# Four p_k buffers, go_o ahead of gs_t, and a new layout and order around the output stage of a gated S4/SwiGLU layer with its gradients

## The chip, the cores and the metric

The kernel runs on one core of a Trainium2 chip. The metric is the device time of one execution in microseconds, as the median of the runs; a time is compared with that of the kernel before.

## The reference, cut to what matters

The layer normalises u (2048 tokens x 576 channels), sends it through a state-space convolution (a kernel K of 2048 taps for each channel, from 128 complex rates) and through a SwiGLU network (576 to 4608 and back), and multiplies both. Besides the output it returns the gradients of the input and of every parameter.

```
def _A_ref(u, A_re, A_im, B_re, B_im, C_re, C_im, log_dt, Dskip):
    dt = exp(log_dt)[:, None]
    logdA = dt * (A_re + 1j * A_im);  dB = dt * (B_re + 1j * B_im)
    P = exp(logdA[:, :, None] * arange(L))
    K = einsum("dn,dnl,dn->dl", C_re + 1j * C_im, P, dB).real
    y = irfft(rfft(u padded to 2L) * rfft(K padded to 2L))[:L]      # per channel
    return y + u * Dskip

def _B_ref(x, w1, w3, w2):
    return (silu(x @ w1) * (x @ w3)) @ w2

xn = layernorm(A_u)
s = _A_ref(xn, ...)
g = silu(_B_ref(xn, w1, w3, w2))
out = A_u + s * g
# returned: out and the vector-Jacobian product of grad_out for A_u, the eight
# S4 parameters, w1, w3 and w2
```

## The kernel before

**Stages.** Times are those of the profiled execution. A prologue (to some 95 us) normalises and makes tables and exponentials. Then three things run interleaved until some 525 us: the *gates* (72 steps of two token tiles by 512 hidden columns: products with w1 and w3 into pg and pu, Silu, the product h, and stores of g, u and h to H_dram, U_dram, G_dram), the *kernel generation* (36 chunks of 16 channels), and the *convolution* in two halves of the channels. The output stage (`ffn_output`, 496 to some 680 us) multiplies H by w2 for 16 token tiles and forms the output and two gradients of the gating. The backward stage (to some 1345 us) runs 18 groups of 256 hidden columns beside the convolution's gradient; the last stage (`phase6_inputs`) forms the input's gradient for 16 token tiles, with the sums for the parameters (`param_half`) between its products.

**Order.** A framework traces the instructions and orders them for each engine by a priority, which `self.at(us)` sets as a due time, and by the dependences; after that each engine and each DMA queue runs strictly in that order. `issue_after` adds an order on one engine without a wait. The gates are laid among the chunks and the convolution by `gate_time` (due times) and `gate_mark` (the chunk or transform whose products a gate must follow on TensorE). `BACK` places the inverse transforms of the convolution's later blocks behind certain gates.

**Memory.** Pools are stacked: a pool opened where an earlier one was closed takes its bytes, and its tiles wait for the last users of the tiles that lay there. The output stage lies on the bytes of the gates and the convolution, and small `gap` pools shift what follows. For the convolution the stack is, from its floor: spectra of u (u_0 to u_3), of the kernel (k2_0 to k2_3), raw spectra (kraw, two buffers), V (two), cm_t (two), s_t (three), ev (two).

**What the change touches.**
- `kgen_chunk` makes p_k and q_k on DVE and stores them to PZ_dram and Q_dram from SP; p_k comes from a pool of two buffers (`sb`), q_k from one of four (`qvp`). `kgen_sum` sums on TensorE, copies to k_s on ACT and spreads k_s over KT on POOL.
- `conv_half` transforms KT in four blocks (`dft_block`: two products, an ACT copy of one to ev, DVE's sum and difference), multiplies the spectra on DVE into V (`cmul_acc`) and transforms back (`idft_side`).
- In `ffn_output`, `begin` loads a tile of H transposed from SP (hcA, hcB, hcC in turn) by the pieces and gates in `marks` for tiles 0 to 2, and in one piece later; `finish` does the sigmoid and the gradients on DVE: go_o stays in SBUF, gs_t is stored to GS_dram from SP, o0 to the output. `turn_go` transposes go_o on TensorE; the framework placed it by its priority and its inputs.
- `param_half` takes two buffers of et_ps from a pool of three PSUM banks; DVE multiplies and reduces each (L1507, L1510).

Of the kernel before, what the change touches and what calls it, by code (L numbers as in the profile page):

```python
# [17 lines left out]
P = 128  # L18
# [82 lines left out]
class K:  # L101
# [25 lines left out]
    def pool(self, **kw):  # L127
        return self.tc.tile_pool(reuse_waits="tile", **kw)
# [617 lines left out]
    def kgen_chunk(self, ch, E, lhs, SEL, sb, qvp, ps):  # L746
# [17 lines left out]
        q = qvp.tile([P, 2, DC // 2, 2 * BV], BF16, name="q_k")  # L764
        p = sb.tile([P, 4, 2, 4, AV], BF16, name="p_k")
        rows = lambda a_: a_.rearrange("p (g d) -> p g d", g=4)
# [200 lines left out]
    def ssm_conv(self, T0, TC, ps, ps1):  # L967
        with self.pool(name="c_u", bufs=1) as up, \
                self.pool(name="c_k", bufs=1) as kp, \
                self.pool(name="c_raw", bufs=2) as rp, \  # L970
                self.pool(name="c_y", bufs=2) as ypool, \
                self.pool(name="c_tmp", bufs=2) as tp, \
                self.pool(name="c_s", bufs=3) as spool, self.pool(name="c_e", bufs=2) as epool:
            self.s_stores = []
            for h in range(2):
                yield from self.conv_half(h, T0 + TC * h * 92, TC, kp, up, rp, ypool, tp, spool, epool, ps)

# [69 lines left out]
    def gate_mark(self, n):  # L1047
        i = n - self.LEAD
        if i < self.SPAN:
            return int(36 * i / self.SPAN + 0.5) - 1  # L1050
        h, k = divmod(i - self.SPAN, 17)
        return 36 + 8 * h + (-1, -1, 0, 0, 1, 1, 2, 3, 3, 4, 4, 4, 5, 5, 5, 6, 6)[k]

# [97 lines left out]
    def ffn_output(self, T0, TB):  # L1151
# [9 lines left out]
        with ExitStack() as es:  # L1161
# [3 lines left out]
                                                           op("epb"), op("gap5"))  # L1165
            hpc, hpc1, hp, ip4, epc, gap6 = op("hc"), op("hc1"), op("h"), op("st", 3), op("epc"), op("gap6")
            wps = [op(f"w{f}") for f in (24, 28, 32, 0)]
            ipx2 = op("in2x")
            psA, psB, psC = [es.enter_context(self.pool(name="o_ps" + n, bufs=1, space=bass.MemoryType.PSUM, side="right"))
# [3 lines left out]
            gap.tile([P, 5120], BF16, name="o_gap")  # L1173
            for g_, n_ in ((gap2, 128), (gap3, 128), (gap4, 1216), (gap5, 128), (gap6, 1152)):
                g_.tile([P, n_], BF16, name="o_gap2")
# [12 lines left out]
                     [(f, f + 6, 61 + f // 6) for f in range(0, FT, 6)],  # L1188
                     [(FC, FC + 9, 67), (FC + 9, FT, 68), (0, 9, 68), (9, FC, 69)]]
            w2a = self.ktp.tile([P, LT, D], BF16, name="w2a", tag="KT")  # L1190
# [51 lines left out]
            def finish(st):  # L1242
# [12 lines left out]
                got = go_o[:, i, :]  # L1255
                nc.vector.tensor_tensor(out=got, in0=gos[:], in1=e[:], op=ALU.mult)
                gs_t = ip.tile([P, D], BF16, name="gs_t")
                nc.vector.tensor_tensor(out=p4(gs_t[:]), in0=n4(go_t[:]), in1=n4(g[:]), op=ALU.mult)
                nc.sync.dma_start(out=self.GS_dram[:, :, i, :].rearrange("g p d -> p g d"),
                                  in_=gs_t[:].rearrange("p (g d) -> p g d", g=4))  # L1260
                if i >= LT - cfg.KT:
                    nc.scalar.copy(out=self.gs_end[:, i - LT + cfg.KT], in_=gs_t[:, 0:D // 4])
                nc.vector.tensor_tensor(out=n4(g[:]), in0=p4(s_t[:]), in1=n4(g[:]), op=ALU.mult)
                o0 = ip.tile([P, D], BF16, name="o0")
                self.epi.append(nc.vector.tensor_tensor(out=o0[:], in0=g[:], in1=x_t[:], op=ALU.add))
                nc.sync.dma_start(out=self.tok("out_0", i), in_=o0[:])
                if i < LT - 1:
                    self.turn_go(i, pst.tile([P, DT, P], BF16, name="ptr"))

# [13 lines left out]
            for i in range(2, LT):  # L1283
                st = begin(i)
                product(st, 0, FT)
                finish(st)
# [29 lines left out]
    def params_open(self, S_all, ps):  # L1316
        cfg = self.cfg
        self.sums = ExitStack()
        gkp = self.sums.enter_context(self.pool(name="g_k", bufs=1, side="right"))
        self.qp = self.sums.enter_context(self.pool(name="g_q", bufs=2, side="right"))  # L1320
        self.zp = self.sums.enter_context(self.pool(name="g_z", bufs=3, side="right"))
        self.prp = self.sums.enter_context(self.pool(name="g_pr", bufs=1, side="right"))
        self.S_all, self.ps_T = S_all, ps
        self.gz = []
        for i in range(3):
            z = gkp.tile([P, 2, 2, 2, 8, cfg.LT], BF16, name=f"gz{i}")
            self.nc.vector.memset(z[:], 0.0)
            self.gz.append(z)
        self.half = 0
        self.loaded = {}  # L1330

# [163 lines left out]
    def param_half(self, ch, dg, gK, qT, pz):  # L1495
        nc, AV = self.nc, self.cfg.AV
        T = [self.ps_T.tile([P, 2, 2, 2, 2, AV], FP32, name="et_ps") for _ in range(2)]
        for x in range(2):
# [474 lines left out]
    def phase6_inputs(self, T2, TX, wT, acts, pool):  # L1973
# [7 lines left out]
        with pool(name="l_sb", bufs=2) as sb, pool(name="l_s1", bufs=1) as s1, \  # L1981
                pool(name="l_sm", bufs=4) as sm, pool(name="x_ps", bufs=2, space=bass.MemoryType.PSUM) as ps:
            def rows(i, gxs, go_o1, queue):
# [262 lines left out]
```

## Time and profile before

| | us |
|---|---|
| median of three runs | 1682.55 |
| the runs | 1669.41, 1682.55, 1689.53 |
| the profiled execution | 1682.95 |
| its span, first to last instruction | 1681.0 |
| PE busy | 1577.1 (94%) |
| DVE busy | 1389.3 (83%) |
| ACT busy | 837.3 (50%) |

How to read the rows: an instruction row begins with its start and its length in us, counted from the span's start, then the engine (PE is TensorE's products, PEld its weight loads, DVE VectorE, ACT ScalarE, POOL GpSimd, SPq the queue of SyncE), the line of the kernel, output <- input with shapes, and xN for N merged into one row. In square brackets stand the idle time of that engine just before and what ended it. A row of the list of waits gives the total, the number and the longest. A row of the table by windows gives the stretch, its length, the busy time of each engine with the number of instructions, the clock granted to TensorE (1.00 is full), the share of the 16 DMA engines and the GB/s moved.

### The profile page before, as it was taken

To read this page: it belongs to the slowest core of one execution; us is meant where nothing else is said; L and a number is where in the kernel's file an instruction comes from. 1 tells how busy PE (TensorE), PEld (TensorE's weight loads), DVE (VectorE), ACT (ScalarE), POOL (GpSimd) and SP (SyncE) were. 2 spreads that over 40 slices of the span, in tenths; PEclk is the share of its full clock that TensorE was granted. 3 is DMA by queue.
4 is the path that set the end of the run, shared out by engine and by line. 5 is a ranking of instruction groups with operands and counts; after the bars stand their busy time and mean duration, and the time that the engine had idled before them with its cause. 6 is when DMAs were issued, how large, how long until landed. Compare 5 with 4: busy or idle time off the path is not lost. (4 is left out here: it accounts for less than half of the span.)

```text
span 1681.0 us, 34288 instructions
## 1 busy us (share of the span) xinstructions
PE 1577.1 (94%) x13275; PEld 1148.2 (68%) x13327; DVE 1389.3 (83%) x2150; ACT 837.3 (50%) x1517; POOL 475.4 (28%) x778
## 2 busy tenths in 40 slices
PE   5799989899997899999999999999999999999998
PEld 2454434344445677788888888888888877887876
DVE  9889988798973455798996999879999964788887
ACT  6789989666652112765656565556555401000001
POOL 7756756533242111011111111111111232213131
PEclk9999999999999999999999999999999999999999
DMA  7899999989799889758676665789999999999993
GB/s 238 298 337 368 376 347 383 322 271 310 246 212 220 213 195 218 229 168 244 189 181 203 199 198 159 213 227 284 247 240 239 234 243 227 252 226 238 243 208 75
DMA packets 621037, 408.57 MB, mean 243 GB/s; under 512 B 424554, under 2 KB 562234, under 8 KB 616266
## 3 DMA queue, kind: packets, MB, share of 16 engines
q1 hardware_dynamic: 565184, 274.01, 64.7%
q0 software_dynamic: 33472, 114.23, 21.0%
q10 hardware_dynamic: 22218, 18.14, 3.8%
q8 instruction: 104, 1.70, 0.4%
q14 instruction: 59, 0.48, 0.1%
HBM read 128.52 MB, written 189.06 MB: 189 GB/s over the span
## 5 line engine op out<-in xcount | busy, mean ns | idle before, releaser
L1948 PEld LDWEIGHTS <-xn_bf 128*128 128x128 bf16 x2304 | 224.4, 98 | 34.7 <-issue 8.5
L2002 PEld LDWEIGHTS <-acts 128*128 128x128 bf16 x1970 | 192.1, 98 | 47.9 <-issue 0.2
L1112 PEld LDWEIGHTS <-xnT 128*128 128x128 bf16 x1152 | 108.3, 98 | 139.2 <-issue 33.3
L1507 DVE TENSOR_TENSOR pr_q<-et_ps,pz 128x1024 f32<-128x1024 f32 x144 | 176.0, 1222 | 29.1 <-PE et_ps L1502 19.9
L1933 POOL DMA_DIRECT2D out_dram<-gw x72 | 47.2, 656 | 536.4 <-ACT gw L1950 310.0
L1510 DVE TENSOR_REDUCE S_all<-pr_q 128x32 f32<-128x1024 f32 x144 | 175.3, 1217 | 3.2
L1882 PE MATMUL ph<-w2T,goT 128*128 128x256 bf16 x1440 | 169.7, 273 | 1.6 <-ACT gh L1885 1.6
L1112 PE MATMUL pg<-wmB_w,xnT 128*128 128x512 bf16 x541 | 151.3, 381 | 13.4 <-DVE g_t L1131 11.3
L2002 PE MATMUL px<-wT,acts 128*128 128x288 bf16 x1242 | 161.0, 287 | 0.0
L1923 PE MATMUL pgw<-go_o,h_n 128*128 128x288 bf16 x1152 | 152.3, 286 | 1.1 <-ACT gw L1929 1.0
L1882 PEld LDWEIGHTS <-goT 128*128 128x128 bf16 x1440 | 139.2, 98 | 18.9 <-issue 3.1
L1112 PE MATMUL pu<-wmB_w,xnT 128*128 128x512 bf16 x566 | 151.3, 385 | 0.3
L1948 PE MATMUL pgw<-gu_n,xn_bf 128*128 128x256 bf16 x1152 | 133.5, 272 | 3.6 <-ACT gw L1929 3.1
L1923 PEld LDWEIGHTS <-h_n 128*128 128x128 bf16 x1152 | 111.9, 98 | 29.2 <-issue 2.1
L1948 PE MATMUL pgw<-gg_n,xn_bf 128*128 128x256 bf16 x1152 | 130.2, 273 | 0.4 <-ACT gw L1950 0.4
L1127 ACT ACTIVATE s_t<-pg 128x512 bf16<-128x512 f32 x144 | 88.2, 612 | 72.3 <-PE pu L1121 59.0
L1885 ACT CAST gh<-ph 128x512 bf16<-128x512 f32 x144 | 80.6, 589 | 82.6 <-PE ph L1882 75.3
L806 POOL COPY KT<-k_s 64x128 bf16<-64x128 bf16 x144 | 87.1, 605 | 57.2 <-ACT k_s L803 52.5
L2121 ACT ACTIVATE go<-gx 128x576 bf16<-128x576 f32 x15 | 10.2, 683 | 178.2 <-DVE gx L2071 169.4
L2002 PE MATMUL px<-wA,acts 128*128 128x288 bf16 x728 | 95.6, 287 | 0.0
L1132 ACT CAST u_t<-pu 128x512 bf16<-128x512 f32 x144 | 87.1, 605 | 7.7 <-PE pu L1112 7.2
L1141 POOL DMA_DIRECT2D G_dram<-g_t x72 | 51.5, 715 | 120.2 <-ACT g_t L1129 75.3
(331 smaller groups left out, 3196.5 us busy)
## 6 DMA issues: line engine op xcount, KB each, us to landing
H_dram<-h_t SPq DMA_DIRECT2D x72, 256.0 KB
U_dram<-u_t POOLq DMA_DIRECT2D x72, 256.0 KB, 5.7
G_dram<-g_t POOLq DMA_DIRECT2D x72, 256.0 KB, 5.2
Q_dram<-q_k SPq DMA_DIRECT2D x36, 512.0 KB
gg_n<-G_dram POOLq DMA_DIRECT2D x18, 1024.0 KB, 6.3
h_n<-U_dram POOLq DMA_DIRECT2D x18, 1024.0 KB, 8.7
GG_dram<-gg_n SPq DMA_DIRECT2D x36, 512.0 KB
GU_dram<-gu_n SPq DMA_DIRECT2D x36, 512.0 KB
```

Source lines behind the costliest of these rows:

```text
L806: nc.gpsimd.tensor_copy(out=KT[64 * hf:64 * hf + 64, :, ch // 9, h, d1:d1 + 8], in_=ks[64 * h:64 * h + 64, :, h, hf].rearrange("p d a -> p ...
L1112: ins = nc.tensor.matmul(pt[:], lhsT=xnT[:, c, ts], rhs=wm[w][:, c, :], start=(q == 0 and c == 0), stop=(q == 1 and c == nfull - 1))
L1127: nc.scalar.activation(out=s_t[:, :, q, :], in_=pgv, func=ACT.Silu)
L1132: self.gate_last = nc.scalar.copy(out=u_t[:, :, q, :], in_=puv)
L1141: self.u_stores[step] = nc.gpsimd.dma_start(out=dst[fb * ng:(fb + 1) * ng, :, i0:i0 + NT, :].rearrange("g p t f -> p g (t f)"), in_=src[:] ...
L1507: nc.vector.tensor_tensor(out=pr[:].rearrange("p r k e -> p r (k e)"), in0=T[x][:].rearrange("p z k h j a -> p (z k h j a)")[:, None].to_b ...
L1510: nc.vector.tensor_reduce(out=self.S_all[:].rearrange("p r (h c) -> p r h c", h=2)[:, :, :, d0:d0 + 2], in_=pr[:].rearrange("p r k (h j a) ...
L1882: self.pe_last = nc.tensor.matmul(ph[j][:, k, :].rearrange("p (a f) -> p a f", f=P), lhsT=lw, rhs=rh, start=(n == 0), stop=(n == nfull))
L1885: self.sc(lambda: nc.scalar.copy(out=gh[:, j], in_=ph[j][:]))
L1923: self.pe_last = nc.tensor.matmul(pgw[pi_][:, 0:pw], lhsT=hn[:, tt, fl * P:(fl + 1) * P], rhs=go_o[:, tt, po:po + pw], start=(tt == 0), st ...
L1948: self.pe_last = nc.tensor.matmul(pw_[:, 0:FG], lhsT=self.xn_bf[:, tt, c * P:(c + 1) * P], rhs=nat[:, tt, :], start=(tt == 0), stop=(tt == ...
L2002: self.pe_last = nc.tensor.matmul(px[pi_][:, 0:pw], lhsT=acts[i][:, ai, fi, :], rhs=w[:, po:po + pw], start=(n == 0), stop=(n == len(steps ...
```

## The change

Four places are edited together. p_k comes from the pool of four buffers. The second half of the convolution is due 88 instead of 92 units after the first, and the gates beside it follow a transform one step later in its list. In `ffn_output` the pools are ordered anew, so that hcB lies on the bytes of kraw and tile 2's two halves on those of V; the pieces of tile 2 follow gates 67, 68, 70 and 71; DVE makes go_o before gs_t and gs_t before the product for the output; and go_o of a tile is transposed after 19 of the 36 steps of the next tile (tiles 0 and 1 after 12 and 25 steps of tile 2). In the last stage every fourth et_ps comes from a PSUM bank of its own.

```
@@ kgen_chunk
-        p = sb.tile([P, 4, 2, 4, AV], BF16, name="p_k")
+        p = qvp.tile([P, 4, 2, 4, AV], BF16, name="p_k")
@@ ssm_conv
-                yield from self.conv_half(h, T0 + TC * h * 92, TC, kp, up, rp, ypool, tp, spool, epool, ps)
+                yield from self.conv_half(h, T0 + TC * h * 88, TC, kp, up, rp, ypool, tp, spool, epool, ps)
@@ gate_mark
-        return 36 + 8 * h + (-1, -1, 0, 0, 1, 1, 2, 3, 3, 4, 4, 4, 5, 5, 5, 6, 6)[k]
+        return 36 + 8 * h + (-1, -1, 0, 0, 1, 1, 2, 3, 3, 4, 4, 4, 5, 5, 5, 6, 6, 6)[k + h]
@@ ffn_output
-            hpc, hpc1, hp, ip4, epc, gap6 = op("hc"), op("hc1"), op("h"), op("st", 3), op("epc"), op("gap6")
+            epc, ipx2, gap6, hp, hpc, hpc1, ip4 = op("epc"), op("in2x"), op("gap6"), op("h"), op("hc"), op("hc1"), op("st", 3)
             wps = [op(f"w{f}") for f in (24, 28, 32, 0)]
-            ipx2 = op("in2x")
...
-            for g_, n_ in ((gap2, 128), (gap3, 128), (gap4, 1216), (gap5, 128), (gap6, 1152)):
+            for g_, n_ in ((gap2, 128), (gap3, 128), (gap4, 1216), (gap5, 128), (gap6, 704)):
...
-                     [(FC, FC + 9, 67), (FC + 9, FT, 68), (0, 9, 68), (9, FC, 69)]]
+                     [(0, 9, 67), (9, FC, 68), (FC, FC + 9, 70), (FC + 9, FT, 71)]]
...
-                nc.vector.tensor_tensor(out=got, in0=gos[:], in1=e[:], op=ALU.mult)
+                made = nc.vector.tensor_tensor(out=got, in0=gos[:], in1=e[:], op=ALU.mult)
                 gs_t = ip.tile([P, D], BF16, name="gs_t")
-                nc.vector.tensor_tensor(out=p4(gs_t[:]), in0=n4(go_t[:]), in1=n4(g[:]), op=ALU.mult)
+                with self.tc.issue_after(made.ins):
+                    made = nc.vector.tensor_tensor(out=p4(gs_t[:]), in0=n4(go_t[:]), in1=n4(g[:]), op=ALU.mult)
...
-                nc.vector.tensor_tensor(out=n4(g[:]), in0=p4(s_t[:]), in1=n4(g[:]), op=ALU.mult)
+                with self.tc.issue_after(made.ins):
+                    nc.vector.tensor_tensor(out=n4(g[:]), in0=p4(s_t[:]), in1=n4(g[:]), op=ALU.mult)
...
-                if i < LT - 1:
-                    self.turn_go(i, pst.tile([P, DT, P], BF16, name="ptr"))
+
+            def turn(i, after):
+                self.turn_go(i, pst.tile([P, DT, P], BF16, name="ptr"), after)
...
-                product(st, 0, FT)
+                f0 = 0
+                for k, f1 in ((0, 12), (1, 25)) if i == 2 else ((i - 1, 19),):
+                    turn(k, product(st, f0, f1))
+                    f0 = f1
+                product(st, f0, FT)
@@ params_open
+        self.ps_X = None
@@ param_half
-        T = [self.ps_T.tile([P, 2, 2, 2, 2, AV], FP32, name="et_ps") for _ in range(2)]
+        T = [(self.ps_X if self.ps_X and (2 * self.half + x) % 4 == 3 else self.ps_T).tile([P, 2, 2, 2, 2, AV], FP32, name="et_ps")
+             for x in range(2)]
@@ phase6_inputs
-                pool(name="l_sm", bufs=4) as sm, pool(name="x_ps", bufs=2, space=bass.MemoryType.PSUM) as ps:
+                pool(name="l_sm", bufs=4) as sm, pool(name="x_ps", bufs=2, space=bass.MemoryType.PSUM) as ps, \
+                pool(name="x_T", bufs=1, space=bass.MemoryType.PSUM) as self.ps_X:
```

## The prediction

> **What bounds the kernel now.** I read the page first, then the table by windows, then all idle time of PE in order of time, then the engine or queue behind each gap. The page says how much TensorE (PE) works.
>
> ```profile
> span 1681.0 us, 34288 instructions
> PE 1577.1 (94%) x13275; PEld 1148.2 (68%) x13327; DVE 1389.3 (83%) x2150; ACT 837.3 (50%) x1517; POOL 475.4 (28%) x778
> ```
>
> The windows (span, then busy time of PE, PEld, DVE, ACT, POOL, PE's granted clock, DMA share, GB/s) separate the stages:
>
> ```profile
> 126.00:336.00 210.00, 196.91 (x1372) 88.07 (x1394) 182.90 (x292) 181.58 (x362) 133.13 (x208) 0.98 1.03 359
> 252.00:294.00 42.00, 41.55 (x294) 18.50 (x298) 36.51 (x58) 39.11 (x79) 26.52 (x43) 1.00 1.03 383
> 328.00:406.00 78.00, 76.03 (x406) 34.30 (x410) 76.20 (x112) 53.54 (x112) 27.98 (x40) 1.00 0.93 294
> 418.00:491.00 73.00, 68.06 (x361) 30.79 (x365) 72.12 (x104) 48.90 (x102) 24.77 (x36) 1.00 0.77 252
> ```
>
> PE is the bound wherever it isn't kept waiting (41.55 of 42 us), so a PE gap that goes away shortens the kernel by its length, unless another engine is late next. In the convolution DVE is as full (76.20 of 78, 72.12 of 73), and in the kernel generation the DMA share is 1.03. I sort the edits by the gap that each can close. Second price of a gap: PE's clock halves behind it.
>
> ```profile
> 228.40:231.70 3.30, 3.30 (x17) 0.94 (x15) 2.89 (x6) 1.76 (x4) 0.72 (x1) 0.50 1.03 400
> ...
> 324.00:327.30 3.30, 3.30 (x12) 0.96 (x10) 0.83 (x2) 0.33 (x1) 2.09 (x3) 0.50 0.87 306
> 491.30:494.50 3.20, 3.20 (x14) 1.89 (x13) 1.47 (x4) 1.35 (x3) 2.13 (x3) 0.50 1.16 78
> 508.40:515.00 6.60, 3.36 (x15) 2.12 (x16) 2.03 (x3) 0.00 (x0) 4.21 (x6) 0.50 1.07 237
> 549.30:556.00 6.70, 4.45 (x21) 2.81 (x22) 3.53 (x6) 0.74 (x2) 1.61 (x3) 0.50 1.16 296
> 1634.70:1638.00 3.30, 3.30 (x16) 2.09 (x14) 3.07 (x4) 0.00 (x0) 0.90 (x2) 0.50 1.28 207
> ```
>
> PE's busy time in such a stretch, halved, is what the clock costs: 1.65 us at 228, 297 and 324 (three alike), 1.6 at 491, 1.7 at 508, 2.2 at 549, 1.65 at 1634. The Trainium skill ("TensorE: Matmul & The Clock Gate", section "Why this matters for your kernels") advises to keep idle gaps of PE under about 3 us, since a window of idle time halves the clock. By it the gaps of 2.09, 2.43 and 2.94 us below would be free of that price, and the sum would come to 1656; the trace halves the clock behind each of the three, so the rows are used.
>
> **1. Four p_k buffers.** p_k moves from a pool with two buffers to one with four.
>
> ```profile
> 212.87 0.81 PE L1112 MATMUL pg<-wmB_w,xnT 128*128 128x512 bf16 x3 [2.24 <-DVE g_t L1131]
> 227.38 0.81 PE L1112 MATMUL pg<-wmB_w,xnT 128*128 128x512 bf16 x3 [3.18 <-DVE g_t L1131]
> 296.06 0.92 PE L1112 MATMUL pg<-wmB_w,xnT 128*128 128x512 bf16 x3 [2.09 <-DVE g_t L1131]
> 323.06 0.59 PE L1112 MATMUL pg<-wmB_w,xnT 128*128 128x512 bf16 x2 [3.21 <-DVE g_t L1131]
> ```
> ```profile
> DVE p_k L767 <- DMA PZ_dram<-p_k: 9.5, 5, 2.5
> ```
> ```profile
> 222.81 0.69 DVE L767 TENSOR_TENSOR p_k<-cp_k,E_l 128x1024 bf16<-128x1024 bf16 x1 [2.76 <-ACT u_t L1132]
> ```
>
> PE waits for DVE to empty pg (g_t), and each of the four times DVE had just waited at L767 for the store of p_k two chunks back (the one at 222.81 is put down to an ACT copy that was already over; I count it with the five). Gaps 2.24 + 3.18 + 2.09 + 3.21 = 10.7 us, three half-clock stretches 5.0: ceiling 15.7. The store itself doesn't get faster; two more chunks of patience must be enough, and behind p_k stand E_l (four buffers, loaded ahead) and h_t (three). With a DMA share of 1.03 a part will come back there. Bounds 0 and 15.7; I take 9.
>
> The Trainium skill ("DMA: Bandwidth & Descriptors", "Where 436 GB/s comes from") puts the limit of HBM for one core at about 358 GB/s. By it this stage (359) could not go faster and the edit would bring nothing, 1660 in all; the row at 252 shows 383 for 42 us, so the trace doesn't agree with it as a ceiling. The mechanism stays as a rival.
>
> **2. Price of that move in SBUF.** The pools of the kernel generation grow by 4 x 2048 - 2 x 2048 = 4096 bytes, so by adding the tile sizes k_s shifts from 132608..134656 to 136704..138752 (counted from the floor that both stages share with the gates). The convolution's second ev buffer lies at 136704..137856: until now on free bytes, afterwards on k_s, whose last reader is POOL.
>
> ```profile
> 332.22 2.91 POOL L806 COPY KT<-k_s 64x128 bf16<-64x128 bf16 x4
> ```
> ```profile
> 329.01 0.45 DVE L903 TENSOR_TENSOR k<-et_ps,ev 128x288 bf16<-128x288 f32 x1
> ```
>
> The second pair of spectra (DVE, 329.0) would come after 335.1: some 6 us later, of which DVE fills about one with h_t. Queued behind the waiting ev copy on ACT are the gates' s_t, g_t, u_t. DVE is full from there to 406, so it isn't made up. Bounds 0 (the scheduler reuses the first ev buffer) and -8; I take -5.
>
> **3. Second half of the convolution sooner (L976, L1052).** Its last inverse transform stays behind gate 69 (BACK), its DVE work starts one gate earlier.
>
> ```profile
> 414.82 0.69 DVE L1135 TENSOR_TENSOR h_t<-s_t,u_t 128x1024 bf16<-128x1024 bf16 x1 [3.75 <-ACT u_t L1132]
> ```
> ```profile
> 490.89 0.86 PE L945 MATMUL et_ps<-V,cT 128*128 128x288 bf16 x4 [2.43 <-DVE V L963]
> ```
>
> DVE idles 3.75 us just before that half; filled, V is 3.75 us sooner, more than the 2.43 that PE waits. Gain 2.43 + 1.6 = 4.0; bounds 0 and 4.0, I take 4.
>
> **4. Layout and order in ffn_output.** By adding tile sizes, tile 1's H (hcB) lay partly on a V buffer; it now covers exactly the two kraw buffers, whose last reader ends before 442. Its six loads may so follow gates 61 to 66 instead of standing behind tile 2's.
>
> ```profile
> 440.95 0.75 DVE L914 TENSOR_TENSOR k<-kraw 128x1152 bf16<-128x1152 bf16 x1
> ```
>
> ```profile
> 443.79 36.43 SPq L1138 DMA_DIRECT2D H_dram<-h_t  x8
> ...
> 491.26 6.79 SPq L1803 DMA_TRANSPOSE hcC<-H_dram  x2
> 498.16 18.22 SPq L1803 DMA_TRANSPOSE hcB<-H_dram  x6
> ...
> 527.21 8.80 SPq L1803 DMA_TRANSPOSE hcA<-H_dram  x1
> ```
> ```profile
> 511.64 3.80 PE L1238 MATMUL po<-w2g,hcB 128*128 128x288 bf16 x16 [6.76 <-DMA hcB<-H_dram]
> 541.30 2.13 PE L1238 MATMUL po<-w2g,hcA 128*128 128x288 bf16 x16 [1.36 <-DMA hcA<-H_dram]
> 551.55 0.86 PE L1293 MATMUL ptr<-ident_bf,go_o 128*128 128x128 bf16 x5 [5.30 <-DVE go_o L1256]
> ```
> ```profile
> 548.73 0.76 DVE L1258 TENSOR_TENSOR gs_t<-go_t,g 128x576 bf16<-128x576 bf16 x1 [6.46 <-DMA GS_dram<-gs_t]
> ```
>
> First gap: 6.76 + 1.7 = 8.5 us, which I take whole, since the eight H stores leave SP nearly empty from 443 to 480. The next two, 1.36 + 5.30 + 2.2 = 8.9, hang on SP's queue: GS stores stand behind the full-tile transposes, gs_t has two buffers, and go_o stood behind gs_t. With go_o first, go_o no longer waits for that store. But tile 3's load must now come sooner, as the products before it do, behind tile 2's last two pieces. Bounds -4 and 8.9; I take 6.
>
> **5. go_o first, the transposes by hand.** The steady output tiles:
>
> ```profile
> 577.72 2.12 PE L1238 MATMUL po<-w2g,hcA 128*128 128x288 bf16 x16
> 579.68 2.98 PE L1238 MATMUL po<-w2a,hcA 128*128 128x288 bf16 x23
> 582.93 0.57 PE L1293 MATMUL ptr<-ident_bf,go_o 128*128 128x128 bf16 x5 [0.27 <-DVE go_o L1256]
> 583.43 1.28 PE L1238 MATMUL po<-w2a,hcA 128*128 128x288 bf16 x9
> ...
> 587.48 1.76 PE L1238 MATMUL po<-w2g,hcB 128*128 128x288 bf16 x13
> ```
> ```profile
> 580.12 0.75 DVE L1258 TENSOR_TENSOR gs_t<-go_t,g 128x576 bf16<-128x576 bf16 x1
> ...
> 582.12 0.75 DVE L1256 TENSOR_TENSOR go_o<-gos,e 128x576 bf16<-128x576 f32 x1
> ```
>
> A tile takes 587.48 - 577.72 = 9.76 us. 16 products take 1.96, so 72 take 8.82, the five transposes 0.50: 0.44 is lost waiting for go_o. Two DVE operations of 0.67 leave go_o's way, so it ends at 581.5; 38 products in, at 582.4, PE asks for it. The same gap comes 11 times (563 to 661): 4.8 us. gs_t and its store come 1.3 us later, hidden behind the next tile's products; if that cover is gone, as after the last tile, it may cost 1. Bounds 3.5 and 4.8; I take 4.8.
>
> **6. A fourth buffer for et_ps in the last stage (x_T).**
>
> ```profile
> 1534.13 0.38 PE L1502 MATMUL et_ps<-gz,qT 128*128 128x128 bf16 x4 [1.14 <-DVE pr_q L1507]
> 1633.59 0.38 PE L1502 MATMUL et_ps<-gz,qT 128*128 128x128 bf16 x4 [2.94 <-DVE pr_q L1507]
> ```
>
> 1.14 + 2.94 + 1.65 = 5.7 at most; DVE must still do the same reductions: 3 to 5.7, I take 5.
>
> **Sum.** 9 - 5 + 4 + 8.5 + 6 + 4.8 + 5 = 32.3 us off the profiled execution's 1682.95 (span 1681.0 and 1.95 around it): 1651. That execution stands 0.4 us from the median of the three runs, 1682.55, whose spread (1669.41 to 1689.53) is about 1%: less than 1% can't be told from no change.
>
> **Rivals.** (a) The DMA engines bound the kernel generation: the wait goes from p_k to E_l or h_t, term 1 is 0, 1660. For it: share 1.03, 359 GB/s; against: 383 at 252. Chance 0.2. (b) The load chain behind tile 2 takes tile 4's gain back: term 4's second part is -4 and a half-clock stretch of 1.7 is added, 1663. For it: one hcA load held SP 8.80 us; against: DMA has more room once hcB is gone from 498 on. Chance 0.15. (c) The change doesn't do what it says: hcB's loads still stand late on SP; 8.5 and 6 are lost, 1666. Chance 0.1. (d) Slower: the six loads that took 18.22 us of SP now stand between the H stores. Eight stores in 36.43 us are 4.55 a gate; three h_t buffers cover two gates, 9.1 us. If a stretch of loads holds SP for longer, DVE stands still on h_t, and DVE is the bound there: 18.2 - 9.1 = 9.1, again 13.6 - 9.1 = 4.5 with tile 2's four pieces, 1.6 of clock. With terms 1 and 3 gone, 2 at -8 and 4's second part at -4: 8.5 - 4 + 4.8 + 5 - 8 - 15.2 = -8.9, 1692. Against it: a piece held SP some 3 us, and gates lie between. Chance 0.05.
>
> **How the numbers follow.** The forecast, 1651, has 0.5. All ceilings with term 2 at 0 give 47.6, 1635; (a), (b) and (c) reach to 1666, and with the low ends of their other terms to some 1672. Range 1636 to 1672. 1% under the profiled time is 1666: the forecast and most of (a) and (b) lie below it, 0.78; within 1% 0.17; slower by over 1%, 0.05.
>
> **What would show it.** No wait of L767 for PZ_dram and no PE gap over 1 us before 330; the second ev copy behind KT's last copy; no PE gap at the last V; hcB's loads on SP before 490 and no gap at its first product; output tiles of 9.3 us; no pr_q wait over 1 us after 1500. A stop of DVE or ACT on E_l, h_t or g_t in its place, or a longer one for hcA, would make the forecast wrong.

## The result, and the profile after

| | before | after |
|---|---|---|
| median of four runs each, us | 1684.93 | 1662.09 |
| the runs | 1669.41 to 1689.53 | 1656.60, 1656.96, 1667.21, 1675.49 |
| the profiled execution: span | 1681.0 | 1673.7 |

The ratio is 0.9897 (95% interval 0.9849 to 0.9946): 1.0% faster. A later comparison gave 0.9886 (0.9836 to 0.9936), with twelve executions of the changed kernel from 1649 to 1701 us. The ratios leave out executions over 1.5% above the fastest of their kernel, seven of those twelve among them, while medians, lowest and highest are of all: there 1677.84 us against 1679.84 for before, only 0.1% apart. The profile shown is of the slowest of the first four, with a stop in it that point 8 below is about.

The page of the changed kernel, and its table by windows (the first three windows as shown for before, the fourth is the output stage):

```profile
span 1673.7 us, 34331 instructions
PE 1579.0 (94%) x13327; PEld 1149.9 (69%) x13327; DVE 1391.2 (83%) x2150; ACT 837.0 (50%) x1517; POOL 472.4 (28%) x778
```
```profile
126.00:336.00 210.00, 199.37 (x1395) 88.33 (x1393) 182.18 (x290) 183.17 (x365) 132.04 (x211) 0.98 1.03 360
328.00:406.00 78.00, 71.54 (x388) 32.58 (x388) 74.29 (x109) 49.51 (x103) 21.69 (x31) 1.00 0.97 298
418.00:491.00 73.00, 70.93 (x388) 33.04 (x388) 68.41 (x99) 48.03 (x100) 29.79 (x44) 1.00 0.95 280
500.00:660.00 160.00, 153.47 (x1242) 118.80 (x1241) 93.32 (x135) 36.67 (x68) 29.20 (x52) 0.99 0.95 221
```

PE is busier where its gaps were closed (199.4 for 196.9 us in the kernel generation, 70.9 for 68.1 in the second half of the convolution), but less busy at 328 to 406 (71.5 for 76.0): gaps have moved there. The DMA share in the kernel generation is 1.03 as before. In the output stage PE is busy 153.5 us at a clock of 0.99; before had there:

```profile
500.00:660.00 160.00, 143.07 (x1109) 106.33 (x1110) 77.77 (x115) 26.71 (x55) 29.28 (x51) 0.96 0.99 206
```

By how much the same instruction comes earlier in the profile after (kps are the sums of a chunk on PE, V the first product of the spectra, ph products of the backward stage):

| instruction | before | after | lead |
|---|---|---|---|
| first kps (no edit acts yet) | 109.57 | 108.13 | 1.4 |
| last kps of the kernel generation | 327.54 | 318.05 | 9.5 |
| first V on DVE | 333.52 | 331.96 | 1.6 |
| first output product | 496.24 | 488.11 | 8.1 |
| first product of hcB | 511.64 | 498.09 | 13.6 |
| sigmoid of output tile 2 | 540.03 | 529.63 | 10.4 |
| sigmoid of output tile 3 | 558.43 | 539.64 | 18.8 |
| sigmoid of output tile 14 | 665.89 | 642.20 | 23.7 |
| PE's wait in front of ph | 680.45 | 656.62 | 23.8 |
| wait for pr_q near 1330 | 1332.18 | 1324.01 | 8.2 |
| end of the span | 1681.0 | 1673.7 | 7.3 |

The lead grows to 23.8 us at the end of the output stage and falls to 8.2 at one place in the backward stage, which no edit touches. The PE gaps of the changed kernel that answer to those of before or are new and over 2 us, in order of time (timeline of PE; the wait of some 3 us for acts near 1370 and that of some 2 us for gz near 1405 are in both kernels):

```profile
275.95 1.86 PE L1112 MATMUL pu<-wmB_w,xnT 128*128 128x512 bf16 x4 [3.49 <-DMA wmB_w<-in_B_w_dram]
...
334.11 0.42 PE L898 MATMUL et_ps<-KT,fT 128*128 128x288 bf16 x2 [2.65 <-DVE k L905]
...
484.25 2.30 PE L945 MATMUL et_ps<-V,cT 128*128 128x288 bf16 x16 [0.59 <-DVE V L963]
...
512.59 0.65 PE L1237 MATMUL po<-w2g,hcA 128*128 128x288 bf16 x4 [3.38 <-DMA w2g<-in_B_w_dram]
...
534.71 0.57 PE L1299 MATMUL ptr<-ident_bf,go_o 128*128 128x128 bf16 x5 [0.51 <-DVE go_o L1255]
...
1258.07 3.31 PE L1956 MATMUL pgw<-gu_n,xn_bf 128*128 128x256 bf16 x16 [14.22 <-ACT gw L1937]
...
1652.69 0.60 PE L1595 MATMUL et_ps<-ident_f,ST 128*64 128x128 f32 x4 [3.36 <-DVE ST L1581]
```

Of before's gaps, 6.76 on hcB, 1.36 on hcA and 2.94 on pr_q are gone, those on V and go_o are down to 0.59 and 0.51, and of the four on g_t two short ones are left (0.92 at 232.25, 1.19 at 244.84). New are 3.49 on a weight load, 2.65 on k, 3.38 on w2g (a part of w2), 14.22 on gw and 3.36 on ST, and two shorter ones on V in the first half of the convolution (1.30 at 381.47, 1.83 at 403.49). Behind the first of them the clock is halved for 5 us (a row of the table by windows):

```profile
276.00:281.00 5.00, 5.00 (x28) 1.90 (x28) 1.29 (x2) 1.66 (x3) 0.45 (x2) 0.50 1.03 403
```

### The profile page after: what moved, and what is told of

It is laid out like the page before. It is cut to its first block, busy times and chain, and to the rows that moved or that the text cites. A ratio compares the mean times of both kernels' runs of the same rounds, so it can differ in the third digit from the quotient of the medians.

```text
span 1673.7 us, 34331 instructions
## 1 busy us (share of the span) xinstructions
PE 1579.0 (94%) x13327; PEld 1149.9 (69%) x13327; DVE 1391.2 (83%) x2150; ACT 837.0 (50%) x1517; POOL 472.4 (28%) x778
## 5 line engine op out<-in xcount | busy, mean ns | idle before, releaser
L1956 PEld LDWEIGHTS <-xn_bf 128*128 128x128 bf16 x2304 | 225.1, 98 | 50.6 <-issue 23.7
L1112 PE MATMUL pg<-wmB_w,xnT 128*128 128x512 bf16 x576 | 156.7, 381 | 3.2 <-DVE g_t L1131 2.7
```

Source lines behind the costliest of these rows:

```text
L1112: ins = nc.tensor.matmul(pt[:], lhsT=xnT[:, c, ts], rhs=wm[w][:, c, :], start=(q == 0 and c == 0), stop=(q == 1 and c == nfull - 1))
L1956: self.pe_last = nc.tensor.matmul(pw_[:, 0:FG], lhsT=self.xn_bf[:, tt, c * P:(c + 1) * P], rhs=nat[:, tt, :], start=(tt == 0), stop=(tt == ...
```

## The experiments

Each table entry is the ratio to the kernel before, with its interval, and the median of all executions; the kernel before had medians of 1678.06 to 1679.99 in these comparisons. Differences under half a per cent are within these intervals, so the mechanisms are read from the profiles, one for each kernel.

| kernel | ratio | median, us |
|---|---|---|
| changed kernel again | 0.9886 (0.9836 to 0.9936) | 1677.84 |
| changed, ev moved | 0.9915 (0.9880 to 0.9950) | 1665.11 (one execution of 7382.89, not explained) |
| changed, s_t loads later | 0.9895 (0.9863 to 0.9928) | 1661.73 |
| before with p_k, ev moved | 1.0069 (1.0037 to 1.0102) | 1691.50 |
| changed, spectra moved | 0.9926 (0.9891 to 0.9962) | 1670.42 |
| changed without x_T | 0.9929 (0.9893 to 0.9964) | 1670.78 |
| changed without go_o first | 0.9964 (0.9934 to 0.9994) | 1677.44 |
| before with the layout alone | 0.9972 (0.9922 to 1.0021) | 1694.75 |
| changed, gg_n on SP | 0.9874 (0.9834 to 0.9914) | 1659.20 |
| changed, spectra moved, s_t loads later | 0.9868 (0.9822 to 0.9915) | 1659.43 |
| changed, spectra moved, gg_n on SP | 0.9881 (0.9828 to 0.9933) | 1662.28 |
| before with gg_n on SP | 0.9991 (0.9950 to 1.0031) | 1679.88 |

**1. The changed kernel again.**

> The changed kernel as it is, once more. Its first profile had one stop that no step of the prediction holds: PE idle 14.22 us at 1258 because ACT waited 13.96 us for a load of G, and a half-clock stretch of 13.65 us (6.8 us lost) behind it: 21 us in all, while its lead over the profile of before fell from 23.4 to 8.2 us. Theory: that stop belongs to one run. The new profile has no gap over 3 us between 1240 and 1270, the lead at 1330 is 20 us or more, and the time is 1655 to 1662, that is 0.983 to 0.988 of before. Rival: the change puts it there (loads that now start together). Then it is there again, and the time is 1670 or more.

The stop was there again, 8.28 us at 1260.58, and that execution took 1681.5 us: against the theory that it belongs to one run. (The expectation priced it too high: the half clock fell mostly into the idle time, so the first profile lost 14.22 + 1.5 us.) The lead was smaller ahead of it, too: a wait of 5.52 us at 651.85 for e is new in this profile, and PE reached ph at 665.40, not 656.62. Five of the twelve executions lie between 1649.1 and 1670.1, which leaves little room for such stops. Point 8 looks for what decides.

**2. What takes the kernel generation's gain: ev moved.** As predicted an ev copy on ACT came only behind POOL's last copy into KT (the first copy, not the second as I had it). ACT shows no wait there; copies for the gates stood in front of it:

```profile
322.73 1.73 POOL L806 COPY KT<-k_s 64x128 bf16<-64x128 bf16 x4
```
```profile
325.37 0.47 ACT L901 COPY ev<-et_ps 128x288 f32<-128x288 f32 x1
```

```
-                self.pool(name="c_s", bufs=3) as spool, self.pool(name="c_e", bufs=2) as epool:
+                self.pool(name="c_e", bufs=2) as epool, self.pool(name="c_s", bufs=3) as spool:
```

> The changed kernel with the two pools c_s and c_e in the other order, so that neither ev buffer lies on k_s. Theory (term 2): the first ev copies no longer wait for POOL's last copy into KT, and the lead of 9.5 us at the end of the kernel generation, which fell to 1.7 by the first pair of spectra, is kept in part: 4 to 8 us less than the changed kernel. Rival: DVE is full in the first half of the convolution (74.3 of 78 us), so it arrives at the same time at the V products however early the spectra start: within 1.5 us of the changed kernel.

Neither. The first ev copy came at 320.28, ahead of POOL's last copy at 333.77, and yet the work behind it was later. The timelines of DVE and of PE in this kernel:

```profile
330.00 0.46 DVE L903 TENSOR_TENSOR k<-et_ps,ev 128x288 bf16<-128x288 f32 x1 [8.76 <-DMA Q_dram<-q_k]
```
```profile
330.88 0.42 PE L898 MATMUL et_ps<-KT,fT 128*128 128x288 bf16 x2 [4.44 <-DVE k L905]
```

DVE stood still for 8.76 us in front of the first spectra, for the store of q_k into Q_dram. The spectra k2_0 lie on bytes of the kernel generation as well, and a q_k that DVE finished by 317.87, and whose store SP issued at 321.64 at the latest, frees them only at 330. In the changed kernel the late ev copy stands behind more gates in the order, and no wait for the store is left in front of the spectra at 326.54. There DVE stood idle for other reasons: 3.95 and 3.38 us for u_t of those gates (until 321.49 and 325.56) and 2.82 us for the load of u in front of the first V.

**3. The same on before: p_k by itself,** with ev off k_s (the edit to p_k of the change and the one of point 2).

> The kernel before with four p_k buffers alone, and c_s and c_e in the other order so that ev does not lie on k_s: term 1 without term 2. Theory: the gaps of 10.7 us before 330 and their half-clock stretches go, and 7 to 11 us of it reach the end: 1672 to 1676. Rival: DVE, full in the convolution, gives it back there: 3 us or less.

```profile
329.11 0.46 DVE L903 TENSOR_TENSOR k<-et_ps,ev 128x288 bf16<-128x288 f32 x1 [10.12 <-DMA Q_dram<-q_k]
```

The last kps came 6.6 us earlier (320.99), and DVE then waited 10.12 us for the same store: first spectra at 329.11 against 328.27 in before. The span is 1682.9 us, against 1681.0 in before. The rival's size holds, not its cause: alone, this edit gains nothing. That the executions are 0.7% slower the one profile doesn't show, and it stays open.

**4. Spectra moved as well.**

```
-                self.pool(name="c_k", bufs=1) as kp, \
-                self.pool(name="c_raw", bufs=2) as rp, \
                 self.pool(name="c_y", bufs=2) as ypool, \
                 self.pool(name="c_tmp", bufs=2) as tp, \
-                self.pool(name="c_s", bufs=3) as spool, self.pool(name="c_e", bufs=2) as epool:
+                self.pool(name="c_raw", bufs=2) as rp, \
+                self.pool(name="c_k", bufs=1) as kp, \
+                self.pool(name="c_e", bufs=2) as epool, self.pool(name="c_s", bufs=3) as spool:
```

> The changed kernel with the convolution's pools in another order: c_k above c_raw, c_y and c_tmp in its place, c_e ahead of c_s. Neither ev nor the first spectra k then lie on a buffer of the kernel generation that is still being stored. With ev alone moved (the run before) DVE stood still for 8.76 us in front of the first spectra until a store of q_k into Q_dram had landed (330.0), and PE for 4.44 us; the second convolution half began at 410.0 instead of 404.2. Theory: what takes back the gain of the kernel generation is that store, through the memory that k shares with q_k. With k elsewhere the first product of k on DVE starts before 324, and the second half begins at 400 or earlier, 4 us or more ahead of the changed kernel. Rival: DVE is full from 328 to 406 or V, which now lies on q_k, waits instead: the second half begins at 403 to 406.

```profile
314.91 0.44 DVE L903 TENSOR_TENSOR k<-et_ps,ev 128x288 bf16<-128x288 f32 x1
...
325.63 1.36 DVE L956 TENSOR_TENSOR V<-u,k 128x2304 bf16<-128x2304 bf16 x1 [2.40 <-DMA u<-UH_dram]
```
```profile
645.77 1.47 PE L1890 MATMUL ph<-w2T,goT 128*128 128x256 bf16 x12 [1.57 <-ACT gh L1893]
```

The theory holds in this profile: first spectra at 314.9 (326.5 in the changed kernel), first ev copy after 395 us at 398.5 (404.2), and 10.9 us of lead over the changed kernel in front of ph (645.77 against 656.62). The median of its executions doesn't show it (1670.42, the changed kernel's twelve 1677.84 and first four 1662.09); the profiled one, with a wA load of 15.6 us in it (point 8), took 1656.26. In two more kernels with the same pools DVE waited longer for the first load of u, and the gain was gone:

```profile
330.62 1.36 DVE L956 TENSOR_TENSOR V<-u,k 128x2304 bf16<-128x2304 bf16 x1 [4.68 <-DMA u<-UH_dram]
```
```profile
331.87 1.36 DVE L956 TENSOR_TENSOR V<-u,k 128x2304 bf16<-128x2304 bf16 x1 [5.67 <-DMA u<-UH_dram]
```

So V starts when u has landed, at 325.6, 330.6 and 331.9 in three executions, and at 332.0 in the changed kernel. What differs is when SP issues that load, behind the stores of the last chunks: at 317.78 in the first, at 322.32, 322.73 and 322.93 in the others; V follows 7.9 to 9.1 us later each time. Behind the store of q_k stands a load, and the load stands behind stores on SP. Why the stores were done sooner in the first was not found; that the pools are worth 10.9 us rests on that one profile.

**5. The gap on w2g: s_t loads later.** POOL's queue in the changed kernel at that place:

```profile
486.57 1.62 POOL L1228 DMA_DIRECT2D s_t<-S_dram  x3
488.24 1.43 POOL L1203 DMA_DIRECT2D w2g<-in_B_w_dram  x2
...
508.04 1.43 POOL L1203 DMA_DIRECT2D w2g<-in_B_w_dram  x2 [15.37 <-DMA hcC<-H_dram]
```

```
+                    w2_last = ld if fi >= F0 else w2_last
...
-                nc.gpsimd.dma_start(out=s_t[:], in_=self.S_dram[:, i, :])
+                with self.tc.issue_after(w2_last.ins) if i < 3 else nullcontext():
+                    nc.gpsimd.dma_start(out=s_t[:], in_=self.S_dram[:, i, :])
```

> The changed kernel with the loads of s_t for the first three output tiles issued on POOL behind the last load of w2g instead of ahead of it. In the changed kernel the last two loads of w2g start at 508.04, after POOL stood still for 15.37 us, and PE waits 3.38 us for them at 512.59, with a half-clock stretch behind. Theory: what holds them is the three loads of s_t ahead of them, which took 15.5 us to land; with the order turned they start before 495, the gap goes, and the time is 3.4 to 5 us less than the changed kernel. Rival: the transposing loads of hcC fill the DMA engines, or gos on DVE becomes late in its place: no gain, within 1.5 us.

```profile
526.99 2.13 PE L1239 MATMUL po<-w2g,hcA 128*128 128x288 bf16 x16 [1.25 <-DMA hcA<-H_dram]
...
544.43 0.57 PE L1301 MATMUL ptr<-ident_bf,go_o 128*128 128x128 bf16 x5 [3.29 <-DVE go_o L1257]
```

The last w2g loads started at 490 and 499 and the gap on them is gone; 1.25 us on hcA and 3.29 on go_o came in its place, and PE reached ph at 658.68 (656.62 in the changed kernel, where the first output product came 1.8 us earlier). That the order of s_t and w2g on POOL decides when w2g is issued is shown; how is not, since the row above puts the end of POOL's wait to a load of hcC. The gain was turned into new waits. Together with point 4:

> The changed kernel with both repairs that gained in their own profile: the convolution's pools in the order c_u, c_y, c_tmp, c_raw, c_k, c_e, c_s, and the loads of s_t for the first three output tiles behind the last load of w2g. With the pools alone the last product of the output tiles ended at 641.8 us instead of 653.8. Theory: both gains are on PE's path, 641.8 or earlier, and the wait for ph's first group comes at 646 or earlier; 1655 to 1668, as the long transposing load falls in or not. Rival: with the pools in that order w2g was no longer late (no gap there in that profile), so the second repair adds nothing: 641 to 643.

(The last products ended at 643.2 and 654.1, not at the 641.8 and 653.8 in it.) PE reached ph at 657.87: neither gain arrived.

**6. The layout alone,** on before: the pools of ffn_output, gap6 and tile 2's gates as in the change.

> The kernel before with term 4 alone: the pools of ffn_output in the new order, gap6 of 704 and the new gates for tile 2's loads. Theory: hcB's loads follow gates 61 to 66, and the gap of 6.76 us and its half-clock stretch at 511 go, 8.5 us; the next two gaps hang on go_o, which is still formed behind gs_t, so only 1 to 4 us of their 8.9 go. 1670 to 1674. Rival: the layout gives the loads their room only together with the earlier second half of the convolution: 3 us or less.

```profile
461.52 7.84 SPq L1802 DMA_TRANSPOSE hcB<-H_dram  x1
...
470.04 8.98 SPq L1802 DMA_TRANSPOSE hcB<-H_dram  x1
...
479.70 6.94 SPq L1802 DMA_TRANSPOSE hcB<-H_dram  x1
```
```profile
DVE h_t L1135 <- DMA H_dram<-h_t: 8.6, 3, 3.9
```
```profile
496.76 1.12 PE L945 MATMUL et_ps<-V,cT 128*128 128x288 bf16 x4 [6.88 <-DVE V L963]
```

hcB's loads do follow the gates and the gap on hcB is gone, but three of the six pieces held SP for 7 to 9 us (the others 1.9 to 5.1), the H stores stood behind them, DVE waited 8.6 us for those, and PE 6.88 us for the last V. This is the prediction's rival (d), in the place and with nearly the price given there for DVE (9.1). A wait for w2g, 3.99 us at 526.10, came behind the gap on hcB here too, as in the changed kernel. The ratio says no gain, but it goes by the four executions between 1665 and 1680; the other seven, the profiled one of 1697 among them, lie between 1691 and 1700, and by the median of all this kernel is 0.9% slower than before (1694.75 against 1679.46). So I take the mechanism from the profile and not the size. In the changed kernel the same pieces took 1.2 to 1.7 us each. The second half of the convolution and its gates stand at other times there; which of the other edits keeps the pieces short was not tried.

**7. go_o first undone, and x_T left out.**

```
-                with self.tc.issue_after(made.ins):
+                if True:
...
+                if i < LT - 1:
+                    self.turn_go(i, pst.tile([P, DT, P], BF16, name="ptr"))
...
-                for k, f1 in ((0, 12), (1, 25)) if i == 2 else ((i - 1, 19),):
-                    turn(k, product(st, f0, f1))
-                    f0 = f1
-                product(st, f0, FT)
+                product(st, 0, FT)
```

> The changed kernel with term 5 undone: on DVE gs_t and g are formed ahead of go_o again, and the transposes of a tile stand where the scheduler puts them. Theory: the steady output tiles take 9.76 us again instead of 9.32, with a wait of 0.27 us for go_o in each, so the output stage from the first product of hcC to the last product of all is 4 to 5 us longer than the changed kernel's 134.2. The wait for go_o near 550 (5.30 us before the change) comes back too: 8 to 12 us in all. Rival: the scheduler orders it as well by itself now that the loads come sooner: 2 us or less.

```profile
581.18 0.57 PE L1297 MATMUL ptr<-ident_bf,go_o 128*128 128x128 bf16 x5 [0.27 <-DVE go_o L1255]
...
590.95 0.57 PE L1297 MATMUL ptr<-ident_bf,go_o 128*128 128x128 bf16 x5 [0.27 <-DVE go_o L1255]
```

The wait of 0.27 us is back in every tile and the tile takes 9.77 us (590.95 - 581.18). From the sigmoid of tile 3 to that of tile 14 it is 107.5 us against 102.6: 4.9, as the theory has it. The other half of the theory fails: the wait for go_o near the start is only 1.37 us (at 532.35), so most of the 5.30 us of before goes without go_o's place (I put it down to the earlier loads), and from the first output product to ph it is 172.0 against 168.5 us, not 8 to 12 more. The profiled execution took 1700.2 us; what makes it so long lies behind ph, PE waits of 19.78 us at 1266.31 and of 7.42 us at 1587.26. The ratio of 0.9964 takes back more than these 3.5 us; that is not explained.

```
-                pool(name="l_sm", bufs=4) as sm, pool(name="x_ps", bufs=2, space=bass.MemoryType.PSUM) as ps, \
-                pool(name="x_T", bufs=1, space=bass.MemoryType.PSUM) as self.ps_X:
+                pool(name="l_sm", bufs=4) as sm, pool(name="x_ps", bufs=2, space=bass.MemoryType.PSUM) as ps:
```

> The changed kernel without the fourth et_ps buffer of the last stage (x_T). The prediction gave it 5 us (bounds 3 to 5.7). Theory now: in the last stage DVE forms pr_q and S_all back to back for each et_ps, so another buffer only moves the wait: the two waits for pr_q after 1500 come back, the wait for ST at the end (3.35 us) gets shorter by as much, and the time from the wait for gz near 1400 to the end of the span is within 1.5 us of the changed kernel's 270.5. Rival: it is 3 us longer or more.

```profile
1529.02 0.38 PE L1510 MATMUL et_ps<-gz,qT 128*128 128x128 bf16 x4 [1.51 <-DVE pr_q L1515]
...
1628.11 0.38 PE L1510 MATMUL et_ps<-gz,qT 128*128 128x128 bf16 x4 [2.58 <-DVE pr_q L1515]
```

The two waits are back, the one for ST at the end is below 1 us, and from the wait for gz (1405.86) to the end of the span (1675.6) it is 269.7 us; in the changed kernel 270.5, in before 269.7. The fourth buffer brings nothing in these profiles. Why is read from DVE in the changed kernel:

```profile
1644.16 1.23 DVE L1515 TENSOR_TENSOR pr_q<-et_ps,pz 128x1024 f32<-128x1024 f32 x1
1645.42 1.22 DVE L1518 TENSOR_REDUCE S_all<-pr_q 128x32 f32<-128x1024 f32 x1
1646.75 1.23 DVE L1515 TENSOR_TENSOR pr_q<-et_ps,pz 128x1024 f32<-128x1024 f32 x1
1648.01 1.22 DVE L1518 TENSOR_REDUCE S_all<-pr_q 128x32 f32<-128x1024 f32 x1
...
1652.25 0.29 DVE L1581 TENSOR_TENSOR ST<-S_all 128x128 f32<-128x128 f32 x1
```

Product and reduction follow each other without a pause, 2.59 us for one et_ps. PE ran ahead by one more buffer and then waited for ST, the last thing that DVE makes of these sums.

**8. The stop near 1258.** ACT waited for the load of gg_n while a transposing load of wA held SP (the timelines of SP, POOL and ACT of the changed kernel):

```profile
1227.72 4.41 SPq L1811 DMA_TRANSPOSE qT<-Q_dram  x1
...
1235.00 24.02 SPq L1811 DMA_TRANSPOSE wA<-in_B_w_dram  x2
```
```profile
1228.62 0.55 POOL L1831 DMA_DIRECT2D gg_n<-G_dram  x1 [0.17 <-issue]
```
```profile
1256.68 1.06 ACT L1858 ACTIVATE gu_n<-gg_n 128x1024 bf16<-128x1024 bf16 x1 [13.96 <-DMA gg_n<-G_dram]
```

The same in before, where the wA load was short:

```profile
1251.81 7.74 SPq L1803 DMA_TRANSPOSE qT<-Q_dram  x1
...
1261.67 4.52 SPq L1803 DMA_TRANSPOSE wA<-in_B_w_dram  x2
```
```profile
1251.79 0.55 POOL L1823 DMA_DIRECT2D gg_n<-G_dram  x1
```

While the wA load ran, the DMA engines were taken up and moved little (rows of the tables by windows, the changed kernel and then before):

```profile
1236.00:1256.00 20.00, 7.85 (x73) 6.62 (x71) 9.34 (x11) 3.90 (x6) 0.55 (x1) 0.78 1.22 88
```
```profile
1262.00:1266.00 4.00, 4.00 (x37) 3.39 (x36) 3.86 (x5) 2.89 (x5) 0.00 (x0) 1.00 0.86 204
```

The share is 1.22 at 88 GB/s, against 0.86 at 204. The Trainium skill ("DMA: Bandwidth & Descriptors", section "Latency and other measured facts") gives 261 GB/s for transposing loads whose middle dimension isn't contiguous; if it held for this load, the bytes of the stretch (88 GB/s for 20 us, other loads among them) would pass in a third of the time, as an estimate. The trace doesn't agree.

```
-        self.gp(lambda: self.nc.gpsimd.dma_start(out=gg[:], in_=self.G_dram[gi]))
+        if gi:
+            self.sp(lambda: self.nc.sync.dma_start(out=gg[:], in_=self.G_dram[gi]))
+        else:
+            self.gp(lambda: self.nc.gpsimd.dma_start(out=gg[:], in_=self.G_dram[gi]))
```

> The changed kernel with the loads of gg_n issued on SP instead of POOL (all groups but the first), so that each stands in a fixed place ahead of the transposing load of wA. In ten profiles so far the wA load near 1240 took 15.6 to 26.7 us in five and 4.2 to 7.1 us in the others. In the three where POOL issued gg_n ahead of the transposing load of qT it was short, in five of the seven where gg_n came 0.4 to 0.9 us behind it, long: an order that a few tenths of a microsecond decide. Theory: with the order fixed no wA load takes over 10 us, PE has no gap over 5 us at 1240 to 1270, and the median falls to 1655 to 1660. Rival: the length doesn't come from that order (the large load and the transposing load slow each other wherever they meet): a gap of 6 to 20 us stays in that place, and the median stays at 1665 to 1678.

```profile
1236.04 0.42 SPq L1832 DMA_DIRECT2D gg_n<-G_dram  x1
1236.51 6.10 SPq L1811 DMA_TRANSPOSE wA<-in_B_w_dram  x2
```

As the theory has it, the wA loads took 6.1 us, PE had no gap over 1 us between 1110 and 1310, and the six executions lie between 1654.2 and 1666.5. Of eleven profiles with gg_n on POOL, gg_n was ahead of qT's load in four (wA 4.2 to 4.6 us) and behind it in seven (15.6 to 26.7 in five, 6.2 and 7.1 in two); with gg_n on SP it was 5.8 to 6.4 in three of three. So a long load came only where gg_n was behind, but two of those seven were short, and on SP gg_n is issued some 4.5 us behind qT's load: what the edit shows is that the long load stays away with gg_n on that queue, not that the order by itself decides. Why the transposing load then runs so slowly was not found.

This stop isn't the only one. Where it is missing, another transposing load was long in two profiles, that of the last output tile's H without x_T, and one of acts in the last stage with ev moved (timelines of SP and PE):

```profile
624.87 22.80 SPq L1811 DMA_TRANSPOSE hcA<-H_dram  x1
```
```profile
659.52 3.90 PE L1237 MATMUL po<-w2g,hcA 128*128 128x288 bf16 x16 [18.47 <-DMA hcA<-H_dram]
```
```profile
1557.51 15.48 SPq L1811 DMA_TRANSPOSE acts<-GU_dram  x1
```
```profile
1571.39 5.17 PE L2011 MATMUL px<-wA,acts 128*128 128x288 bf16 x30 [12.36 <-DMA acts<-GG_dram]
```

These executions took 1677.4 and 1684.6 us without the stop near 1258, so gg_n's place can't account for all the long ones. Whether those stops stay away with gg_n on SP is open. With the spectra of point 4, and on before:

> The changed kernel with two repairs: the convolution's pools in the order c_u, c_y, c_tmp, c_raw, c_k, c_e, c_s, and gg_n loaded on SP. Theory: gg_n on SP alone gave 1659 us; the pools alone let the first product of k start at 314.9 us instead of 326.5 and the wait in front of ph come at 645.8 instead of 656.6 in one profile, but at 657.9 in another, where V waited 4.68 us for the load of u. If the load of u is what is left, V starts at its landing, between 325 and 331, and the time is 1648 to 1659, ahead of gg_n alone by what V is earlier. Rival: the pools bring nothing beyond gg_n: 1657 to 1662.

> The kernel before with the loads of gg_n on SP and nothing else, to see how much of the difference between the two kernels hangs on the long transposing load near 1240. Theory: before has the same load and the same order at stake (in its profile POOL issued gg_n 0.02 us ahead of qT's load, and the wA load was short), so its time falls by less, 0 to 6 us, and its runs draw together: 1671 to 1678; the changed kernel with the same edit, 1659, is then 14 to 19 us ahead, more than the 1.1% between the two kernels as they are. Rival: gg_n on SP gains as much here as it did in the changed kernel (10 us or more): 1665 to 1669, and the distance stays about 1%.

The first was no better than gg_n on SP alone (V waited for u until 331.9). On before the edit changes nothing (0.9991). The theory's 0 to 6 us less holds at its low end, but the runs don't draw together (1667.84 to 1696.83). The two kernels with the edit stand 1659.2 to 1679.9: 1.2% apart by both medians and ratios. No version here is faster than the changed kernel by more than the intervals; the one with gg_n on SP has the narrowest times, from six executions.

## Why the prediction was right or wrong

The time of 1662.09 lies in the range and 11 us above the forecast; a ratio of 0.9897 is at the edge between faster and no change. That it lies there is in part luck: two of the four executions were quick, and the twelve later ones have a median of 1677.84, above the range. In the sum, too, errors cancel: terms 2, 6 and the first part of 4 came out 14.1 us too low in all, term 3 and the second part of 4 gave 5.0 more than put. By its terms, from the table of leads, which is one profile of each kernel:

- **Term 1 (9):** 9.5 - 1.4 = 8.1, well sized. No wait of L767 for PZ_dram is left, and of the four gaps 0.92 and 1.19 us are left. What came back is a new gap of 3.49 us on the weights wmB_w at 275.95 with 2.5 us of half clock: a part of what rival (a) feared, within the stage, but on another load than E_l. The rule of a limit at 358 GB/s, which I had weighed, didn't bind: 276 to 281 ran at 403. The Trainium skill ("Perfetto Trace Analysis", section "Roofline") says that on this chip one core by itself can pull more than that share, which agrees.
- **Term 2 (-5):** 1.6 - 9.5 = -7.9, its low bound. (Measured on V; by then the changed kernel had made one more h_t than before, and PE lost its part later, in the gaps of 2.65, 1.30 and 1.83.) The step that failed is the cause: that ev lies on k_s and comes late I found rightly, but with it taken away (2 and 3) a store, and with that taken away (4) a load stood behind it. So the gain of term 1 is given back at the border of the stage. The store and the load are DMA waits; in the changed kernel itself 2.82 us of DVE's idle time is the load and 7.3 us the gates in front of the late copy. Rival (a) placed such a wait at E_l or h_t inside the stage; it came at the border.
- **Term 3 (4):** 8.1 - 1.6 = 6.6 from the first V to the first output product, of which the gap on V (2.43 to 0.59) and its clock are 3.4. The rest I put down to DVE's slack in this stretch (68.4 busy of 73 for 72.1). No run tried this edit by itself.
- **Term 4 (8.5 + 6):** the first gap went whole, as put; but the step from the gap to the gain failed: the products met w2g's last load 14 us later. 13.6 - 8.1 = 5.4, then 10.4 - 13.6 = -3.2: 2.3 of 8.5. What is late next was not asked, though before shows it: there POOL issued the same loads at 510.80, and PE, held at hcB until 511.64, came to them after they had landed. The second part is 18.8 - 10.4 = 8.4 (6, ceiling 8.9).

```profile
510.80 2.83 POOL L1204 DMA_DIRECT2D w2g<-in_B_w_dram  x4 [14.53 <-DVE gos L1253]
```
- **Term 5 (4.8):** 23.7 - 18.8 = 4.9; tiles of 9.32 us.
- **Term 6 (5):** 0, outside its bounds of 3 to 5.7. "DVE must still do the same reductions" was written and not drawn to its end: DVE is the bound there, so a buffer moves PE's wait only, to ST.
- **What no term held:** the stop of 14.22 us, and stops like it elsewhere (8). The sum of the measured terms is 22.4 of 32.3; with the 1.4 of the start, which no edit makes, it is the lead of 23.8 in front of ph, which would make 1682.95 - 23.8 = 1659; the quicker executions of the first four took 1656.6 and 1657.0.
- **Rival (d)** had 0.05, and the layout alone shows that its mechanism is real; beside the other edits it stayed away, and which of them does that was not tried. The parts are not independent: p_k with ev moved and the layout alone gain nothing on before, and with all the rest they gain 1%.

What was to be seen came true for L767, V, hcB's loads (all six on SP between 454 and 480), the tiles and pr_q after 1500; not for the second ev copy (it was the first), nor for a PE free of waits before 330.

## What to carry to other kernels

When an edit shortens a stage whose DMA share is at 1, look at what its last stores and the next stage's first loads hold up: there the gain is asked back, through memory that tiles share, and taking one such wait away shows the next. Price a buffer by the engine that empties it; if that one runs without a pause, the buffer only moves the wait. Where one kernel's times spread by more than the gain, compare several profiles for a stop that comes and goes, and for issues a few tenths of a microsecond apart that change places; then count how many profiles the order accounts for, and look for the same stop elsewhere.

## What the runs showed of the hardware

A transposing load that took 4.2 to 4.6 us in four profiles took 15.6 to 26.7 in five, in one of them with the DMA engines at a share of 1.22 and 88 GB/s (point 8), and others took 22.8 and 15.5; in the layout alone, three pieces of 1.2 to 1.7 us in the changed kernel took 7 to 9. With ev moved, at a DMA share of 1.04 from 318 to 330, a q_k held its buffer for some 12 us (made by 318, free at 330), at least 8.4 of them after SP had issued the store. The clock halved behind gaps of 3.36 to 3.49 us (0.50 and 0.51 in the stretches behind them), and in before behind 2.09, 2.43 and 2.94; behind the 2.65 us at 334 it did not (328 to 406 at 1.00), nor in before behind the 2.24 us at 212.87 (1.00 from 213 to 216.5).
